# Weight conversions of a second MLP layer tied behind the last input copy, and the last output tile stored in halves on two queues

## Chip, cores and metric

One Trainium2 chip, one core of it. The metric is the device time of one execution in microseconds (us), of which the median of the runs is taken. The engines are TensorE (PE: matmuls; PEld: its weight loads), VectorE (DVE), ScalarE (ACT), GpSimd (POOL), and SyncE (SP), which issues the DMAs. The matrix of PE runs at one of two clock levels, and the profile shows the share that was granted.

## The reference

Attention over 4 batches, 12 heads, 448 positions and 64 channels, with RMS-normed queries and keys, is followed by two MLPs over the 1792 rows. The second MLP is where the change lies. Its weights are float64.

```python
def _moe_ref(x, w_in, w_out, s, b) -> np.ndarray:
    h = x @ w_in
    r = np.maximum(h, 0.0)
    g = s * (r * r) + b
    return (g @ w_out).astype(np.float32)

def _moe2_ref(x, w_in, w_out) -> np.ndarray:
    h = x @ w_in
    g = h * np.cos(h)
    return (g @ w_out).astype(np.float32)
```

Each x is 1792 x 768, each w_in 768 x 2048, each w_out 2048 x 768.

## The kernel before

Every fp32 operand of the MLPs is held as a high and a low part (`wh`, `wl` of a weight, `xh`, `xl` of an input, `gh`, `gl` of an activation), and each product is three matmuls (`products`). The weights come as 64-bit floats. `load_weight` (L435 on) loads each half of a weight, 128 x 384, as raw 64-bit words on SP's queue (L456, L458), takes the words apart with two ACT conversions, `c` (L468) and `t` (L469), joins them with three DVE passes (L472 to L474), casts the high part on ACT and subtracts on POOL (`halves`, L431 and L434). There are two raw buffers, two of `c`, three of `t`, and three of `wh` and of `wl`.

The second layer works in eight chunks of two tiles of the 2048 inner columns. For each tile and each of four batches there is an input unit (`unit_in`, L494 on): 18 matmuls into a PSUM buffer `ph`, of which there are three. ACT copies it out (`hs`, L523), and that frees the buffer; then ACT, DVE and POOL work out g = h cos(h) (`kk` L526 and L527, DVE L529 and L530, `gt` L531 and L532 on ACT and L533 on POOL, `gh` L534, `gl` L535). An output unit (`unit_out_2`, L574 on) is six matmuls of 128 rows by half of the 768 columns into a PSUM buffer `po`, of which there are three too. In the first chunk ACT copies `po` out (L590), in the others DVE adds it to the sum (L592). After the last chunk each of the 14 row tiles is stored (L600), in two pieces, since the rows of a tile lie in two places of the output.

`body` writes the program in the order of a list of units, with the weights `LOOK` = 8 units ahead (`ahead`). A scheduler that follows the dependencies then sets the order of each engine. `issue_after(later, earlier)` adds a dependency for the order alone: no semaphore is added. The first 16 weight halves are held behind certain exponentials of the attention in this way (`gate`); all later ones, those of the second layer among them, had no such tie.

Names in the rows of the order: `hs_2_1` is the copy of inner tile 2, batch 1; `c_4_1_0_1_0` is of segment 4 (the second layer), kind 1 (output weights; 0 is input weights), chunk or tile 0, column half 1, half 0.

Of the kernel before, what the change touches and what calls it, by code (L numbers as in the profile page):

```python
# [33 lines left out]
def body(ctx, tc, q, k, v, g_q, g_k, w1_in, w1_out, s_in, b_in, w2_in, w2_out, out):  # L34
    nc = tc.nc
    B, H, S, D = q.shape
    E = out.shape[1]
    F = w1_in.shape[1]
    P = 128
    NCH = 4  # L40
# [5 lines left out]
    NCK = NF // CF  # L46
    EH = E // 2
    CW = EH
    NT = 2 * S // P
# [35 lines left out]
    marks = {}  # L85
# [5 lines left out]
    def issue_after(later, earlier):  # L91
        info = mybir.DependencyInfo(mybir.DependencyClass.NoSync, mybir.DependencyReason.DATA)
        tc.add_manual_dep(later.ins, earlier.ins.name, info, reason="issue order")
# [342 lines left out]
    def load_weight(key):  # L436
        layer, seg, kind, a, e = key
        w = ((w1_in, w1_out), (w2_in, w2_out))[layer][kind]
        name = "_".join(map(str, key))
        wh = wp.tile([P, 2 * CW], F32R, tag="wh", name=f"wh_{name}", bufs=3)  # L440
        wl = wp.tile([P, 2 * CW], F32R, tag="wl", name=f"wl_{name}", bufs=3)
        weights[key] = wh, wl
        for o in range(2):
            kk = f"{name}_{o}"
            hi_part, lo_part = (z[:, o * CW:(o + 1) * CW] for z in (wh, wl))
            if (layer, kind, a, e, o) in plain:
                t = wp.tile([P, CW], F32, tag="t", name=f"t_{kk}", bufs=3)
                nc.sync.dma_start(t, plain[layer, kind, a, e, o])
                halves(t, hi_part, lo_part, nc.vector)
                continue  # L450
            own = "xb" in pools or count["raw"] % 3 < 2
            raw = (wp if own else pools["att"]).tile([P, CW], I64, tag="raw", name=f"raw_{kk}", bufs=2 if own else 1)
            count["raw"] += 1
            if kind == 0:
                src = w[o * CW:(o + 1) * CW, a * P:(a + 1) * P].rearrange("(c p) f -> p c f", p=P)
                dma = nc.sync.dma_start(raw.rearrange("p (c f) -> p c f", f=P), src)  # L456
            else:
                dma = nc.sync.dma_start(raw, w[(CF * a + o) * P:(CF * a + o + 1) * P, e * CW:(e + 1) * CW])  # L458
            if seg == 0 and kind == 0 and a == 0:
                follow(dma, marks["start"])  # L460
            ru = raw.bitcast(U32).rearrange("p (n two) -> p n two", two=2)
            lo, hi = ru[:, :, 0], ru[:, :, 1]
            c = wp.tile([P, CW], U32, tag="c", name=f"c_{kk}", bufs=2)
            cf = c.bitcast(F32)
            t = wp.tile([P, CW], U32, tag="t", name=f"t_{kk}", bufs=3)
            gate = GATE + 4 * min(count["raw"] - 1, 7) + 2 * max(count["raw"] - 8, 0)
            gate = min(gate, len(exps) - 1) if count["raw"] <= 16 else None
            for z in (nc.scalar.activation(cf, hi.bitcast(F32), AF.Copy, scale=2.0**-112),  # L468
                      nc.scalar.activation(t, lo, AF.Copy, scale=LSCALE, bias=-0.5)):  # L469
                if gate is not None:  # L470
                    issue_after(z, exps[gate])
            nc.vector.tensor_scalar(cf, cf, VMAX, -VMAX, ALU.min, ALU.max)  # L472
            nc.vector.scalar_tensor_tensor(t, c, 0x80000000, t, ALU.bitwise_and, ALU.bitwise_or)  # L473
            nc.vector.scalar_tensor_tensor(t, c, 3, t, ALU.logical_shift_left, ALU.bitwise_or)  # L474
            if layer == 0:
                d = dram.tile([P, CW], F32, tag=f"w_{kk}", name=f"wd_{kk}")
                nc.sync.dma_start(d, t.bitcast(F32))
                plain[layer, kind, a, e, o] = d
            halves(t.bitcast(F32), hi_part, lo_part, behind=exps[gate + 1] if count["raw"] <= 8 and gate + 1 < len(exps) else None)
# [3 lines left out]
    acc = {}  # L483
# [3 lines left out]
    def unit_in(layer, seg, ck, f, b):  # L487
        ft = ck * CF + f
        key = f"{layer}_{ft}_{b}"
        wh, wl = weights[layer, seg, 0, ft, 0]  # L490
        wh, wl = (z.rearrange("p (c f) -> p c f", f=P) for z in (wh, wl))
        pool, tag, bufs = (pools["psb"], "ph", 3) if "psb" in pools else (psm, "mo", 2)
        ph = pool.tile([P, 512], F32, tag=tag, name=f"ph_{key}", bufs=bufs)
        at = span(layer, seg, ck, b)  # L494
        size = at.stop - at.start
        h = ph[:, :size]

        def temp(pool, tag, name):
            return pool.tile([P, WIDE], F32, tag=tag, name=f"{name}_{key}")[:, :size]

        for c in range(NE):
            x = [z[:, at] for z in home(layer, b)[c]]
            for n, (a, m) in enumerate(products((wh[:, c, :], wl[:, c, :]), x)):
                nc.tensor.matmul(h, a, m, start=(c == 0 and n == 0), stop=(c == NE - 1 and n == 2))  # L504
            if c % 2 and c < NE - 1:
                yield 1.13
        if count["g"] % 2 == 0:
            n = count["g"] // 2
            gp, nb = (ma, 3) if "mb" not in pools or n % 5 < 3 else (pools["mb"], 2)
            pair[:] = [gp.tile([P, 2 * S], F32R, tag=f"g{z}", name=f"g{z}_{key}", bufs=nb) for z in "hl"]  # L510
        to = at if wide(layer, seg, ck) else slice(count["g"] % 2 * S, (count["g"] % 2 + 1) * S)
        gh, gl = (z[:, to] for z in pair)
        count["g"] += 1
        if layer == 0:
            r = temp(ma, "t0", "r")
            nc.scalar.activation(r, h, AF.Relu)  # L516
            r2 = temp(pools["mb"], "t1", "r2") if "mb" in pools else r
            nc.gpsimd.tensor_tensor(r2, r, r, ALU.mult)  # L518
            gt = temp(ma, "t2", "gt")
            nc.vector.tensor_scalar(gt, r2, sb[:, 0:1], sb[:, 1:2], ALU.mult, ALU.add)  # L520
        else:
            hs = temp(ma, "t0", "hs")
            nc.scalar.copy(hs, h)  # L523
            h = hs
            kk = temp(pools["mb"], "t1", "kk")
            nc.scalar.activation(kk, h, AF.Copy, scale=1.0 / (2 * math.pi), bias=MAGIC)  # L526
            nc.scalar.activation(kk, kk, AF.Copy, bias=-MAGIC)  # L527
            gt = temp(ma, "t2", "gt")
            nc.vector.scalar_tensor_tensor(gt, kk, -C1, h, ALU.mult, ALU.add)  # L529
            nc.vector.scalar_tensor_tensor(gt, kk, -C2, gt, ALU.mult, ALU.add)  # L530
            nc.scalar.activation(gt, gt, AF.Abs)  # L531
            nc.scalar.activation(gt, gt, AF.Sin, scale=-1.0, bias=halfpi)  # L532
            nc.gpsimd.tensor_tensor(gt, h, gt, ALU.mult)  # L533
        nc.scalar.copy(gh, gt)  # L534
        nc.gpsimd.tensor_tensor(gl, gt, gh.bitcast(F32), ALU.subtract)  # L535
        g[ft, b] = (gh, gl)
        if layer == 1 and b % 2:
            g[ft, "pair", b // 2] = list(pair)
        yield 1.13
# [36 lines left out]
    def unit_out_2(seg, ck, eh, t):  # L576
        key = f"1_{ck}_{eh}_{t}"
        w = [z.rearrange("p (f e) -> p f e", f=CF) for z in weights[1, seg, 1, ck, eh]]
        pr, j0 = t // NT, t % NT * P
        po = po_tile(key)[:, :EH]  # L580
        for f in range(CF):
            x = [z[:, j0:j0 + P] for z in g[ck * CF + f, "pair", pr]]
            for n, (a, m) in enumerate(products(x, [z[:, f, :] for z in w])):
                nc.tensor.matmul(po, a, m, start=(f == 0 and n == 0), stop=(f == CF - 1 and n == 2))  # L584
        if ck == 0 and eh == 0:
            pool, nb = (ma, NE) if t < NE else (pools["mb"], 2 * NT - NE)
            acc[t] = pool.tile([P, E], F32, tag="acc", name=f"acc_{key}", bufs=nb)
        at = acc[t][:, eh * EH:(eh + 1) * EH]
        if ck == 0:
            nc.scalar.copy(at, po)  # L590
        else:
            nc.vector.tensor_tensor(at, po, at, ALU.add)  # L592
        if ck < NCK - 1 or eh == 0:
            return
        j = j0
        while j < j0 + P:
            b, c, p = 2 * pr + j // S, j % S // CP, j % CP
            n = min(CP - p, j0 + P - j)
            rows = out[b * S:(b + 1) * S, :].rearrange("(p c) e -> c p e", c=NCH)[c, p:p + n, :]
            nc.sync.dma_start(rows, acc[t][j - j0:j - j0 + n, :])  # L600
            j += n

    pools["ps"] = att_scope.enter_context(tc.tile_pool(name="ps", bufs=2, space=PSUM))
# [87 lines left out]
    for n, u in enumerate(units):  # L691
# [24 lines left out]
        for cost in (unit_in if u[0] == "in" else unit_out)(*u[1:]):  # L716
            debt += cost * rates[min(seg, 1)]
            while debt > 0:
                c = next(steps, None)
# [34 lines left out]
```

## Time and profile before

| what | us |
|---|---|
| median of 3 runs | 1271.97 (1271.52 to 1272.73) |
| the profiled execution, own time | 1274.62 |
| its span, first to last instruction | 1272.7 |
| PE busy | 1239.8 (97%) |
| DVE, ACT, POOL busy | 854.2, 758.5, 624.7 |

The page of the profile gives the busy time and share of each engine, the chain that ended last and the costliest groups of instructions. Since PE is busy for nearly all of the span, the views to read are those that show where it waits and where its clock is lower. A group's idle time is that of its engine just before it, with what ended the wait.

### The profile page before, as it was taken

The page shows a single profiled execution, that of the slowest core. Times are in us where ns is not written, and L with a number is a line of the kernel's source. Part 1 is how long each engine was busy: PE and PEld are TensorE (multiplying, and loading weights), DVE is VectorE, ACT ScalarE, POOL GpSimd, SP SyncE. Part 2 cuts the span into 40 slices and gives each one's busy share as a digit, 9 for nine tenths or more (in the row PEclk, how much of TensorE's full clock was granted, in tenths as well). Part 3 has the DMA queues.
Part 4 walks back from the last instruction along what each step waited for, and adds up shares of the span by engine and source line. Part 5 has one row for each costly group of instructions (what it writes and reads, how often), then busy time and mean ns, then how long its engine had stood idle before and what let it go on. Part 6 is the DMA issues. An engine that isn't in the chain of part 4 may idle for free.

```text
span 1272.7 us, 19065 instructions
## 1 busy us (share of the span) xinstructions
PE 1239.8 (97%) x6788; PEld 1042.6 (82%) x6788; DVE 854.2 (67%) x1448; ACT 758.5 (60%) x1704; POOL 624.7 (49%) x681
## 2 busy tenths in 40 slices
PE   7999999999999999999999999899999999999998
PEld 5555676676877777889999999799899999999998
DVE  6888778878778674753454447754767766666755
ACT  5777887776667664435332226688656657566741
POOL 4566857575655526434332223555443545354531
PEclk9999999899999999999999999999999999999999
DMA  4323325434334343453222112211112111111105
GB/s 124 103 83 120 114 78 158 146 104 132 117 114 125 101 117 95 143 157 95 83 65 62 51 45 75 75 50 51 53 47 75 50 50 50 50 50 50 53 10 174
DMA packets 82222, 111.33 MB, mean 87 GB/s; under 512 B 8112, under 2 KB 72144, under 8 KB 82128
## 3 DMA queue, kind: packets, MB, share of 16 engines
q1 hardware_dynamic: 82128, 110.13, 28.6%
q8 instruction: 53, 0.87, 0.3%
q14 instruction: 41, 0.34, 0.1%
HBM read 86.51 MB, written 23.59 MB: 87 GB/s over the span
## 4 chain that ended last, share of the span: by engine, by line
PE 64%; DVE 7%; ACT 6%; DMA 2%; POOL 2%; issue 1%; DVEq 0%; ACTq 0%; POOLq 0%
PE ph L504 26%; PE po L558 15%; PE po L584 14%; PE tp L306 3%; PE av L329 3%; PE sc L265 3%; DVE gt L529 1%; DVE t L473 1%; DVE gt L530 1%; DVE t L474 1%; DVE c L472 1%; POOL wl L434 1%; DMA raw<-in_moe_w_out_dram 1%; DMA raw<-in_moe_w_in_dram 1%; DMA xr<-xd 1%
## 5 line engine op out<-in xcount | busy, mean ns | idle before, releaser
L535 POOL TENSOR_TENSOR gl<-gt,gh 128x448 fp32r<-128x448 f32 (+2 forms) x128 | 155.3, 1220 | 155.2 <-ACT gh L534 155.1
L504 PE MATMUL ph<-xha,wh 128*128 128x448 f32 (+2 forms) x576 | 212.3, 371 | 3.6 <-ACT hs L523 3.4
L504 PE MATMUL ph<-xha,wl 128*128 128x448 f32 (+2 forms) x576 | 211.1, 367 | 0.0
L504 PE MATMUL ph<-xla,wh 128*128 128x448 f32 (+2 forms) x576 | 210.7, 367 | 0.0
L434 POOL TENSOR_TENSOR wl<-t,wh 128x384 fp32r<-128x384 f32 x128 | 139.5, 1105 | 61.4 <-ACT wh L431 58.7
L431 ACT CAST wh<-t 128x384 fp32r<-128x384 f32 x200 | 95.6, 512 | 107.9 <-PE po L558 52.2
L566 DVE TENSOR_TENSOR acc<-po,acc 128x448 f32<-128x448 f32 x168 | 103.2, 618 | 83.8 <-PE po L558 83.8
L558 PE MATMUL po<-gh,wh 128*128 128x448 f32 x384 | 145.8, 382 | 8.5 <-DVE acc L566 6.4
L584 PE MATMUL po<-wh,gh 128*128 128x384 f32 x448 | 151.6, 339 | 1.7 <-DVE acc L592 1.5
L584 PE MATMUL po<-wl,gh 128*128 128x384 f32 x448 | 150.1, 335 | 0.4 <-POOL wl L434 0.4
L584 PE MATMUL po<-wh,gl 128*128 128x384 f32 x448 | 150.3, 335 | 0.0
L592 DVE TENSOR_TENSOR acc<-po,acc 128x384 f32<-128x384 f32 x196 | 105.3, 551 | 62.3 <-PE po L584 62.0
L558 PE MATMUL po<-gh,wl 128*128 128x448 f32 x384 | 141.1, 367 | 0.4 <-POOL wl L434 0.4
L287 ACT ACTIVATE pr<-sc,top 112x448 f32<-112x448 f32 x184 | 116.4, 640 | 41.3 <-DVE top L279 40.7
L558 PE MATMUL po<-gl,wh 128*128 128x448 f32 x384 | 140.8, 367 | 0.0
L533 POOL TENSOR_TENSOR gt<-hs,gt 128x512 f32<-128x512 f32 x64 | 76.0, 1194 | 123.8 <-ACT gt L532 115.4
L473 DVE SCALAR_TENSOR_TENSOR t<-c,t 128x384 uint32<-128x384 uint32 x128 | 99.8, 783 | 46.5 <-ACT t L469 43.6
L279 DVE TENSOR_REDUCE top<-sc 112x1 f32<-112x448 f32 x192 | 111.7, 615 | 18.0 <-PE sc L265 17.7
L504 PEld LDWEIGHTS ph<-xha,wh 128*128 128x128 f32 x576 | 108.7, 189 | 17.7 <-ACT hs L523 3.8
L518 POOL TENSOR_TENSOR r<-r 128x448 f32<-128x448 f32 x64 | 63.7, 996 | 120.3 <-ACT r L516 119.6
L534 ACT CAST gh<-gt 128x448 fp32r<-128x448 f32 (+2 forms) x128 | 71.4, 567 | 85.1 <-DVE gt L520 52.2
L504 PEld LDWEIGHTS ph<-xla,wh 128*128 128x128 f32 x576 | 108.6, 189 | 9.0 <-issue 0.6
(109 smaller groups left out, 2701.7 us busy)
## 6 DMA issues: line engine op xcount, KB each, us to landing
raw<-in_moe_w_in_dram SPq DMA_DIRECT2D x64, 384.0 KB, 3.4
raw<-in_moe_w_out_dram SPq DMA_DIRECT2D x64, 384.0 KB, 3.3
t<-wd SPq DMA_DIRECT2D x72, 192.0 KB, 2.4
wd<-t SPq DMA_DIRECT2D x64, 192.0 KB, 2.9
rawk<-in_k_dram SPq DMA_DIRECT2D x24, 224.0 KB, 3.7
rawv<-in_v_dram SPq DMA_DIRECT2D x24, 224.0 KB, 3.0
rawq<-in_q_dram SPq DMA_DIRECT2D x23, 224.0 KB, 3.5
xd<-xf SPq DMA_DIRECT2D x12, 224.0 KB, 3.0
```

The source lines that it names most:

```text
L279: line("DVE", nc.vector.tensor_reduce(tops[j], sc[j], axis=AX.X, op=ALU.max, negate=True))
L287: e = line("ACT", nc.scalar.activation(pr, sc[j], AF.Exp, bias=tops[j], scale=scale[j], accum_out=st[i]["sums"][:, c, j:j + 1]))
L431: z = nc.scalar.copy(wh, w)
L434: eng.tensor_tensor(wl, w, wh.bitcast(F32), ALU.subtract)
L473: nc.vector.scalar_tensor_tensor(t, c, 0x80000000, t, ALU.bitwise_and, ALU.bitwise_or)
L504: nc.tensor.matmul(h, a, m, start=(c == 0 and n == 0), stop=(c == NE - 1 and n == 2))
L533: nc.gpsimd.tensor_tensor(gt, h, gt, ALU.mult)
L535: nc.gpsimd.tensor_tensor(gl, gt, gh.bitcast(F32), ALU.subtract)
L558: marks["out"] = nc.tensor.matmul(po, a, m, start=(f == 0 and n == 0), stop=(f == CF - 1 and n == 2))
L566: nc.vector.tensor_tensor(at, po, at, ALU.add)
L584: nc.tensor.matmul(po, a, m, start=(f == 0 and n == 0), stop=(f == CF - 1 and n == 2))
L592: nc.vector.tensor_tensor(at, po, at, ALU.add)
```

## The change

Two things. First, each ACT conversion of a raw weight that has no other tie is now ordered behind the last `hs` copy that `body` had written until then. Second, the last row tile (t = 13) is stored in column halves: each half after its own last addition, and of its two pieces the first goes on SP's queue and the second on ACT's. Before, it was stored whole after both additions, both pieces on SP's queue.

```diff
@@ -469,6 +469,8 @@
                       nc.scalar.activation(t, lo, AF.Copy, scale=LSCALE, bias=-0.5)):
                 if gate is not None:
                     issue_after(z, exps[gate])
+                elif "hs" in marks:
+                    issue_after(z, marks["hs"])
@@ -520,7 +522,7 @@
             hs = temp(ma, "t0", "hs")
-            nc.scalar.copy(hs, h)
+            marks["hs"] = nc.scalar.copy(hs, h)
             h = hs
@@ -590,14 +592,17 @@
-        if ck < NCK - 1 or eh == 0:
+        closing = t == 2 * NT - 1
+        if ck < NCK - 1 or eh == 0 and not closing:
             return
+        cols = slice(eh * EH, (eh + 1) * EH) if closing else slice(0, E)
         j = j0
         while j < j0 + P:
             b, c, p = 2 * pr + j // S, j % S // CP, j % CP
             n = min(CP - p, j0 + P - j)
-            rows = out[b * S:(b + 1) * S, :].rearrange("(p c) e -> c p e", c=NCH)[c, p:p + n, :]
-            nc.sync.dma_start(rows, acc[t][j - j0:j - j0 + n, :])
+            rows = out[b * S:(b + 1) * S, :].rearrange("(p c) e -> c p e", c=NCH)[c, p:p + n, cols]
+            queue = nc.scalar if closing and j > j0 else nc.sync
+            queue.dma_start(rows, acc[t][j - j0:j - j0 + n, cols])
             j += n
```

The order of the four engines is as before up to the border of the two layers. Lines after L471 have moved by two, and those after L593 by up to five.

ACT at the border, before: the copy `hs_0_2` and what stands ahead of it.

```order
L534 CAST gh_1_0_9042<-gt_1_1_9135 128x384
L469 ACTIVATE t_4_1_0_0_1_9169<-raw_4_1_0_0_1_9166 128x384
L469 ACTIVATE t_4_1_0_1_0_9454<-raw_4_1_0_1_0_9451 128x384
L468 ACTIVATE c_4_1_0_1_1_9464<-raw_4_1_0_1_1_9462 128x384
L468 ACTIVATE c_4_0_3_0_0_9613<-raw_4_0_3_0_0_9611 128x384
L523 COPY hs_0_2_9218<-ph_0_2_9197 128x512
```

The same place now:

```order
L431 CAST wh_4_0_2_0_9087<-t_4_0_2_0_0_9092 128x384
L431 CAST wh_4_0_2_0_9087<-t_4_0_2_0_1_9103 128x384
L536 CAST gh_1_0_9042<-gt_1_0_9049 128x512
L109 CAST xha_96<-acc_0_5_2_7263 128x448
L533 ACTIVATE gt_1_1_9135<-gt_1_1_9135 128x384
L469 ACTIVATE t_4_1_0_0_1_9169<-raw_4_1_0_0_1_9166 128x384
L534 ACTIVATE gt_1_1_9135<-gt_1_1_9135,halfpi 128x384
L536 CAST gh_1_0_9042<-gt_1_1_9135 128x384
L525 COPY hs_0_2_9218<-ph_0_2_9197 128x512
```

Three conversions have left the place ahead of `hs_0_2`; one, `t_4_1_0_0_1`, stands two places further ahead, and the `wh` casts stand ahead of both `gh`.

POOL at the same place, now:

```order
L535 TENSOR_TENSOR gt_1_0_9049<-hs_1_0_9044,gt_1_0_9049 128x512
L434 TENSOR_TENSOR wl_4_0_2_0_9088<-t_4_0_2_0_0_9092,wh_4_0_2_0_9087 128x384
L434 TENSOR_TENSOR wl_4_0_2_0_9088<-t_4_0_2_0_1_9103,wh_4_0_2_0_9087 128x384
L537 TENSOR_TENSOR gl_1_0_9043<-gt_1_0_9049,gh_1_0_9042 128x512
L535 TENSOR_TENSOR gt_1_1_9135<-hs_1_1_9130,gt_1_1_9135 128x384
```

Before, `gl_1_0` and `gt_1_1` stood ahead of the two `wl`.

ACT behind the copy of unit (2, 1), now, where the conversions that were ahead of `hs_0_2` stand (`acc<-po` are the copies out of PSUM):

```order
L525 COPY hs_2_1_9382<-ph_2_1_9363 128x384
L468 ACTIVATE c_4_1_0_1_0_9453<-raw_4_1_0_1_0_9451 128x384
L469 ACTIVATE t_4_1_0_1_0_9454<-raw_4_1_0_1_0_9451 128x384
L468 ACTIVATE c_4_1_0_1_1_9464<-raw_4_1_0_1_1_9462 128x384
L469 ACTIVATE t_4_1_0_1_1_9465<-raw_4_1_0_1_1_9462 128x384
L528 ACTIVATE kk_2_0_9352<-hs_2_0_9350 128x512
L592 COPY acc_0_0_4_9438<-po_0_0_4_9431 128x384
L528 ACTIVATE kk_2_1_9384<-hs_2_1_9382 128x384
L529 ACTIVATE kk_2_0_9352<-kk_2_0_9352 128x512
L431 CAST wh_4_1_0_1_9449<-t_4_1_0_1_0_9454 128x384
L592 COPY acc_0_0_5_9447<-po_0_0_5_9440 128x384
```

Before, `hs_2_1` was followed by `kk_2_0`, the copy of `po_0_0_6` and the rest of `kk`, with no conversion among them.

## Rows read from the trace of the kernel before

**Rows 1.** The page, part 1: PE's busy time, share, instructions.

```profile
PE 1239.8 (97%) x6788; PEld 1042.6 (82%) x6788; DVE 854.2 (67%) x1448; ACT 758.5 (60%) x1704; POOL 624.7 (49%) x681
```

**Rows 2.** Table by stretch: length, busy time of engines, granted clock (PEclk), DMA.

```profile
800.00:820.00 20.00, 16.62 (x79) 14.24 (x78) 15.55 (x22) 12.45 (x26) 10.46 (x9) 0.97 0.15 41
820.00:840.00 20.00, 20.00 (x102) 18.82 (x101) 15.20 (x20) 17.23 (x38) 10.82 (x9) 0.94 0.27 79
840.00:860.00 20.00, 20.00 (x109) 19.05 (x109) 9.08 (x12) 17.85 (x41) 12.87 (x12) 1.00 0.15 41
```

**Rows 3.** Waits of PE from 800 us: total, times, longest.

```profile
PE ph L504 <- ACT hs L523: 3.4, 1, 3.4
PE po L584 <- DVE acc L592: 1.5, 3, 0.7
PE po L584 <- POOL wl L434: 0.4, 1, 0.4
```

**Rows 4.** Timeline of PE, the hole: start, us, what, idle before.

```profile
815.62 0.40 PE L504 MATMUL ph<-xla,wh 128*128 128x512 f32 x1
819.40 0.69 PE L504 MATMUL ph<-xha,wh 128*128 128x384 f32 x1 [3.38 <-ACT hs L523]
...
822.43 0.34 PE L504 MATMUL ph<-xha,wh 128*128 128x384 f32 x1
...
822.78 0.33 PE L504 MATMUL ph<-xla,wh 128*128 128x384 f32 x1
```

**Rows 5.** Timeline of ACT ahead of the late copy.

```profile
811.84 0.51 ACT L534 CAST gh<-gt 128x384 fp32r<-128x384 f32 x1
...
814.03 0.56 ACT L469 ACTIVATE t<-raw 128x384 uint32<-128x384 uint32 x1 [0.80 <-POOL wl L434]
816.48 0.55 ACT L468 ACTIVATE c<-raw 128x384 f32<-128x384 f32 x1 [1.89 <-DMA raw<-in_moe_w_out_dram]
818.33 0.54 ACT L468 ACTIVATE c<-raw 128x384 f32<-128x384 f32 x1 [1.30 <-DMA raw<-in_moe_w_in_dram]
818.78 0.57 ACT L523 COPY hs<-ph 128x512 f32<-128x512 f32 x1
```

**Rows 6.** Timeline of POOL at the same time.

```profile
810.26 1.02 POOL L533 TENSOR_TENSOR gt<-hs,gt 128x384 f32<-128x384 f32 x1 [2.70 <-ACT gt L532]
811.24 2.76 POOL L434 TENSOR_TENSOR wl<-t,wh 128x384 fp32r<-128x384 f32 x2
813.96 1.34 POOL L535 TENSOR_TENSOR gl<-gt,gh 128x384 fp32r<-128x384 f32 x1
```

**Rows 7.** Timeline of PE: one of the small waits.

```profile
969.40 0.45 PE L584 MATMUL po<-wh,gh 128*128 128x384 f32 x1 [0.68 <-DVE acc L592]
```

**Rows 8.** Table by stretch: the stretch with that wait.

```profile
950.00:1000.00 50.00, 49.32 (x264) 46.25 (x263) 35.01 (x64) 32.22 (x62) 22.41 (x20) 1.00 0.19 59
```

**Rows 9.** Groups from 816 to 1268 us: count, busy, mean ns, idle before, releasers.

```profile
L468 ACT ACTIVATE c<-raw 128x384 f32<-128x384 f32 x55 | 30.3, 551 | 31.5 <-DMA raw<-in_moe_w_out_dram 13.2 <-DMA raw<-in_moe_w_in_dram 7.3 <-DVE t L474 4.8
L473 DVE SCALAR_TENSOR_TENSOR t<-c,t 128x384 uint32<-128x384 uint32 x56 | 46.8, 836 | 30.5 <-ACT t L469 29.1
```

**Rows 10.** Timeline of ACT: a copy out of PSUM in the first chunk.

```profile
848.87 0.47 ACT L590 COPY acc<-po 128x384 f32<-128x384 f32 x1
```

**Rows 11.** Timeline of PE: the next use of that PSUM buffer.

```profile
851.05 0.33 PE L584 MATMUL po<-wh,gh 128*128 128x384 f32 x1
```

**Rows 12.** The page, part 6: loads of raw weights, KB, us to landing.

```profile
raw<-in_moe_w_in_dram SPq DMA_DIRECT2D x64, 384.0 KB, 3.4
```

**Rows 13.** Timeline of DVE: the last addition.

```profile
1268.00 0.56 DVE L592 TENSOR_TENSOR acc<-po,acc 128x384 f32<-128x384 f32 x1 [0.48 <-PE po L584]
```

**Rows 14.** Timeline of SP's queue: the first store after it.

```profile
1268.59 0.31 SPq L600 DMA_DIRECT2D out_dram<-acc  x1
```

**Rows 15.** DMA issues from 1266 us: count, KB, us to landing.

```profile
out_dram<-acc SPq DMA_DIRECT2D x1, 336.0 KB, 2.8
out_dram<-acc SPq DMA_DIRECT2D x1, 96.0 KB, 1.8
```

## The prediction

> **What bounds the kernel now.** I read the shares of the engines first. TensorE (PE) is busy for 1239.8 of the 1272.7 us [rows 1], so only what makes PE wait, or run slower, or what lies outside its work, can be won. Next I read the table by stretch across the border of the two layers. From 800 to 820 us PE is busy 16.62 of 20 us, and from 820 to 840 it is busy throughout, but at a granted clock of 0.94 and with 102 matmuls, where the next 20 us hold 109 [rows 2]. Then the list of who waited for whom, from 800 us on: one wait of 3.4 us for `hs` on ScalarE (ACT), three of 1.5 us together for VectorE (DVE), one of 0.4 us for GpSimd (POOL) [rows 3]. So the second layer has one large hole, and the timeline shows it: PE starts a matmul at 815.62 and the next at 819.40, with 3.38 us idle; nine starts later, at 822.43, full pace is back [rows 4].
>
> The hole has two prices. The wait itself is 3.38 us. After it the nine matmuls from 819.40 to 822.43 take 3.03 us, where two later starts from 822.43 to 822.78 are 0.175 us apart, so nine should take 1.58: 1.45 us more. Their pace is that of the lower of the two clock levels (1.2 against 2.4 GHz). Together **4.83 us**.
>
> Why `hs` is late stands on ACT's own timeline [rows 5]. The cast `gh` ends at 812.35. Then four conversions of weights stand ahead of `hs`: two wait for POOL (they start at 814.03 at the latest), two for a load of raw weights (1.89 and 1.30 us of idle time; they start at 816.48 and 818.33), and `hs` starts only at 818.78. ACT works in order, so a copy that frees a PSUM buffer for PE stands behind transfers that it does not need.
>
> **The change, part by part.**
>
> *The tie.* Every layer-two conversion now stands behind the last `hs` written ahead of it. By the order of instructions, one conversion is left between the `gh` work and the `hs` in question, and it waits for POOL's earlier casts alone; the two that waited for loads are gone from there. What is late next is POOL: its new order puts both `wl` and a `gl` ahead of the `gt` that the last `gh` ahead of `hs` needs. If the pair starts where it did, at 811.24, then 2.76 (pair) + 1.34 (`gl`) + 1.02 (`gt`) [rows 6] end at 816.4; `gh` and `hs` add 0.51 and 0.57 [rows 5], so `hs` ends at 817.4. PE is free at about 816.0. That leaves 1.4 us of the wait. The `wh` casts that release the pair stand two places earlier on ACT now, worth 2 × 0.5, so 0.4 is left; at best it is nothing. I take 0.7, between 0.4 and 1.4 and nearer to the lower, and assume that the clock holds: the wait of 0.68 us at 969.40 lies in a stretch with a granted clock of 1.00 [rows 7, 8]. Won: 4.83 − 0.7 = **4.1 us**; ends 4.83 (no wait) and 3.38 − 1.4 = 2.0 (the clock falls all the same).
>
> *What is now behind the tie.* Of the conversions that were done before the hole, four now come after `hs` of unit (2, 1), in the stretch in which ACT also empties the output units' PSUM buffers (28 copies by the code, first chunk only). Each is 0.55 us [rows 9]: 2.2 us more work for ACT. ACT comes to the first `hs` about 2.7 us sooner (3.38 − 0.7), so it is 0.5 us ahead of the old program, while PE is 4.1 us ahead: PE comes 3.6 us closer to ACT. The cover is the time from a copy's end to the next use of its buffer, three output units on: at the tightest from 849.34 to 851.05, 1.7 us [rows 10, 11]. So 1.9 us would be missing, if ACT had no gaps; it has, 2.8 and 2.15 us in the two stretches of 20 us [rows 2]. Ends 0 and 1.9. I take **0.7 us lost**, nearer to the end with gaps, as a gap that waits for a load stays a gap.
>
> *Loads.* The raw tile has two buffers, so a load on SP's queue starts when the conversions two halves earlier are done. The same loads stand in the same order; they start later, and take 3.4 us [rows 12]. The tightest weight is that for input tile 3: from the matmul that ends unit (2, 1) to its first use PE has 79 matmuls of 384 columns (0.175 us each) and 18 of 512 (by columns 0.233), 18.0 us. The chain: two conversions free the buffer (1.1), load (3.4), four conversions (2.2), three DVE passes (0.84 each at the mean of the slowest kind [rows 9], 2.5), `wh` about 0.5, `wl` pair 2.76: 12.5 us. It is hidden; cost nothing, with 5.5 us to spare.
>
> *The last tile.* Before, DVE's last addition ends at 1268.56, the 48 KB store is issued at 1268.59 for 0.31 us, and the 336 KB one behind it, landing 2.8 us later [rows 13, 14]. Now half of both has left one unit earlier, and the last large store is 168 KB and issued on ACT's queue at once. The place in the queue gives 0.31 us. Landing lies between 1.8 us (96 KB) and 2.8 us (336 KB) [rows 15]; I take 2.2, by size nearer to 96 KB, and so 0.6. Sum **0.9 us**; ends 1.3 (landing as for 96 KB) and −0.3 (all lands as late as before, and a queue unused until then costs one more issue of 0.31). Two more stores are issued beside other work.
>
> The Trainium skill, "DMA: Bandwidth & Descriptors", section "Rules for kernel authors", speaks against this: stores from several engines share the same 16 DMA engines, so a second queue saves issue time alone. By it the tail would give 0.31 us and the sum below would be 3.7; the halving by time, one unit earlier, is a thing it does not speak of.
>
> *The small waits* of 1.5 and 0.4 us [rows 3] depend on DVE's and POOL's order, which moves everywhere in layer two. They may go or come again elsewhere: 0, ends +1.9 and −1.9.
>
> **Sum:** 4.1 − 0.7 + 0.9 = 4.3 us. The profiled execution's own time is 1274.62 (1272.7 of span and 1.9 around it), so it would be 1270.3; that execution is 2.65 us above the median of the runs, and against the median of 1271.97 the forecast is **1267.7 us**.
>
> **Rivals.**
> 1. *ACT becomes the bound in the first chunk.* The copies out of PSUM come late by the whole 3.6 us, because each gap waits for a load as before. For it: ACT is busy 17.23 and 17.85 of 20 us there, without the additions [rows 2]. Against it: PE is busy throughout in both stretches, so there is cover. Time: 4.1 − 3.6 + 0.9 = 1.4 us won, 1270.6.
> 2. *Slower: a weight comes late in every chunk.* In all seven chunks two weights now begin behind the second input copy. For it: the conversions already idle 20.5 us for loads [rows 9], and their cover falls to 18 us. Against it: a chain of 12.5 us. It decides once queueing behind other work on ACT and DVE adds over 5.5 us; at 1.5 us late seven times it costs 10.5 us: 1278.2.
> 3. *The last store lands no sooner after its issue.* The two halves are in flight on the same DMA engines within about one output unit, and the last 168 KB land 2.8 us after their issue, as 336 KB did [rows 15]. For it: size alone does not set the time, since 3.5 times the bytes of the 96 KB store took only 1.0 us more. Against it: the smaller store was the faster all the same. The tail gives the place in the queue, 0.31 us: 3.7 us won, 1268.3. The Trainium skill's rule named above comes to the same.
> 4. *Everything goes:* no wait is left at the hole (4.83), nothing is lost on ACT, tail 0.9, small waits gone (1.9): 7.6 us won, 1264.4.
>
> That the change does nothing is no rival: the order of instructions shows the conversions moved.
>
> **Numbers.** Chances: forecast 0.39, rival 1 0.23, rival 2 0.07, rival 3 0.15, rival 4 0.16. A measurement here tells 0.2% from no change, 2.5 us. Forecast, 3 and 4 lie below 1269.4: faster 0.70. Rival 1 lies within: same 0.23. Slower 0.07. The range leaves out rival 2 and the far side of rival 4, some 0.15, and takes in the bounds of the evacuation, the wait and the tail: 1264.6 to 1270.9.
>
> **What would show it.** Right: no wait for `hs` of over 1 us near 816 us, no stretch at 0.94, `hs` directly behind `gh` on ACT, and less than the 4.1 us (1272.7 − 1268.56) from DVE's last addition to the end. Rival 1 would show as PE waiting for the copies of the first chunk between 830 and 850 us; rival 2 as PE waiting for `wh` or `wl` once in every chunk. The prediction is wrong if the hole keeps over 2 us, or if waits of more than 2 us appear where none are now.

## The result and the profile after

| kernel | median, us | runs | ratio to before, 95% interval |
|---|---|---|---|
| before, beside the changed kernel | 1271.52 | 7 (1270.54 to 1278.24) | |
| changed | 1280.03 | 7 (1278.78 to 1285.55) | 1.0064 (1.0042 to 1.0087) |

The change makes the kernel slower by some 8 us. The forecast was 1267.7 us, its range 1264.6 to 1270.9, so the time lies outside and on the other side.

The profiled execution of the changed kernel has an own time of 1278.78 us, the fastest of its runs; that of before, 1274.62, is 3 us above its median. At the border, up to which the order is the same, the changed execution is already 2.9 us ahead: the first matmul whose place differs starts at 776.86 us in place of 779.76. So the two spans, 1277.0 and 1272.7, understate the loss, and the traces are compared by stretch.

**The hole is gone, as forecast.** First the same table by stretch as before [rows 2], of the changed kernel, from 800 to 860 us:

```profile
800.00:820.00 20.00, 19.82 (x97) 17.37 (x96) 13.60 (x20) 14.84 (x32) 12.23 (x10) 1.00 0.15 41
820.00:840.00 20.00, 20.00 (x110) 19.11 (x109) 11.62 (x20) 19.17 (x43) 10.01 (x10) 1.00 0.26 79
840.00:860.00 20.00, 20.00 (x108) 18.78 (x107) 12.98 (x17) 17.02 (x39) 11.43 (x10) 1.00 0.28 80
```

PE is busy for 19.82 us in place of 16.62, and the granted clock is 1.00 in all three rows. ACT's timeline at that place:

```profile
807.20 0.55 ACT L469 ACTIVATE t<-raw 128x384 uint32<-128x384 uint32 x1
810.63 0.51 ACT L536 CAST gh<-gt 128x384 fp32r<-128x384 f32 x1 [2.38 <-POOL gt L535]
811.05 0.58 ACT L525 COPY hs<-ph 128x512 f32<-128x512 f32 x1
```

`hs` starts directly behind `gh`, which waits for POOL's `gt` alone. Before, `hs` started at 818.78 [rows 5].

**New waits stand in the later chunks.** Whom PE waits for, from 790 us on (total, times, longest); before it was [rows 3]:

```profile
PE po L586 <- DVE acc L594: 7.5, 11, 2.5
PE po L586 <- POOL wl L434: 0.9, 1, 0.9
PE ph L506 <- DVE xla L110: 0.2, 1, 0.2
```

The waits for VectorE's additions have grown from 1.5 us in three to 7.5 us in eleven. The longest, on PE's timeline:

```profile
1142.33 0.34 PE L506 MATMUL ph<-xla,wh 128*128 128x384 f32 x1
1145.16 0.44 PE L586 MATMUL po<-wh,gh 128*128 128x384 f32 x1 [2.50 <-DVE acc L594]
...
1146.66 0.52 PE L586 MATMUL po<-wl,gh 128*128 128x384 f32 x1
...
1149.56 0.52 PE L586 MATMUL po<-wl,gh 128*128 128x384 f32 x1
```

and the table by stretch of what follows:

```profile
1146.00:1150.00 4.00, 4.00 (x16) 3.84 (x15) 3.88 (x6) 1.37 (x5) 2.13 (x2) 0.58 0.00 0
```

PE waits 2.50 us; 1.5 us after it has started again the clock falls, and ten matmuls from 1146.66 on take 0.32 us each in place of 0.174, 1.5 us more. VectorE's timeline tells why the addition was late:

```profile
1139.36 0.54 DVE L594 TENSOR_TENSOR acc<-po,acc 128x384 f32<-128x384 f32 x1
1139.83 0.90 DVE L475 SCALAR_TENSOR_TENSOR t<-c,t 128x384 uint32<-128x384 uint32 x1
1140.76 1.53 DVE L476 SCALAR_TENSOR_TENSOR t<-c,t 128x384 uint32<-128x384 uint32 x1
1142.22 1.16 DVE L474 TENSOR_SCALAR c<-c 128x384 f32<-128x384 f32 x1
1143.49 0.56 DVE L475 SCALAR_TENSOR_TENSOR t<-c,t 128x384 uint32<-128x384 uint32 x1
1144.08 0.56 DVE L476 SCALAR_TENSOR_TENSOR t<-c,t 128x384 uint32<-128x384 uint32 x1
1144.56 0.55 DVE L594 TENSOR_TENSOR acc<-po,acc 128x384 f32<-128x384 f32 x1
```

Five passes of weight conversions stand between two additions, and VectorE has hardly any idle time there (0.2 us). So here no weight is late: the engine that makes the weights is busy with them when it should empty a `po` buffer.

**How much, and where.** I summed over PE's matmuls the time from one start to the next less the matmul's own pace at full clock (0.1735 us for 384 columns, 0.2295 for 512, 0.206 for the few of 448): the lateness, which holds waits, slow clock and slow starts alike.

| stretch, us | 796–880 | 880–940 | 940–1000 | 1000–1060 | 1060–1120 | 1120–1180 | 1180–end | 880–end |
|---|---|---|---|---|---|---|---|---|
| before | 5.4 | 2.8 | 1.5 | 0.3 | 0.3 | 1.3 | 1.2 | 7.3 |
| changed | 0.9 | 2.9 | 4.1 | 1.6 | 2.2 | 4.7 | 4.3 | 19.7 |

The hole gives back 4.5 us, the later chunks lose 12.4. Of the 12.4, listed waits are 6.4 (2.0 to 8.4); each wait also slows the two starts beside it by some 0.27 us together, 2.2 us more for eight more waits; the fall of the clock is 1.5. Of the remaining 2.3, 0.8 are idle times under 0.15 us, thirteen in place of two, which the list of waits leaves out; the rest are slower starts that the profile gives no reason for.

**The tail** is shorter. VectorE's last addition, the last two stores and the landing of the stores (count, KB, median us):

```profile
1273.03 0.56 DVE L594 TENSOR_TENSOR acc<-po,acc 128x384 f32<-128x384 f32 x1 [0.49 <-PE po L586]
1273.61 0.31 SPq L605 DMA_DIRECT2D out_dram<-acc  x1
1273.62 0.38 ACTq L605 DMA_DIRECT2D out_dram<-acc  x1
```

```profile
out_dram<-acc ACTq DMA_DIRECT2D x2, 168.0 KB, 2.4
out_dram<-acc SPq DMA_DIRECT2D x2, 24.0 KB, 2.0
```

From the end of the last addition (1273.58) to the end of the span (1276.99) it is 3.41 us, before 4.19 (1268.56 to 1272.75): 0.78 won. In all, −4.5 + 12.4 − 0.8 = 7.1 us, beside 8.5 by the medians, whose interval is 5.3 to 11.1.

### The profile page after: what moved, and what is told of

Read it like the earlier page. It is cut to its first block, busy times and chain, and to the rows that moved or that the text cites. A ratio compares the mean times of both kernels' runs of the same rounds, so it can differ in the third digit from the quotient of the medians.

```text
span 1277.0 us, 19073 instructions
## 1 busy us (share of the span) xinstructions
PE 1242.4 (97%) x6788; PEld 1041.7 (82%) x6788; DVE 859.4 (67%) x1448; ACT 757.7 (59%) x1704; POOL 627.5 (49%) x681
## 4 chain that ended last, share of the span: by engine, by line
PE 61%; DVE 12%; ACT 6%; issue 2%; POOL 1%; DMA 1%; DVEq 0%; POOLq 0%; ACTq 0%
PE ph L506 24%; PE po L560 16%; PE po L586 12%; PE av L329 3%; PE tp L306 3%; PE sc L265 3%; DVE t L475 2%; DVE t L476 2%; DVE gt L531 2%; DVE c L474 2%; DVE gt L532 1%; DVE acc L594 1%; DMA xr<-xd 1%; ACT gh L536 1%; ACT kk L529 1%
## 5 line engine op out<-in xcount | busy, mean ns | idle before, releaser
L535 POOL TENSOR_TENSOR gt<-hs,gt 128x512 f32<-128x512 f32 x64 | 80.7, 1266 | 124.2 <-ACT gt L534 124.0
L506 PEld LDWEIGHTS ph<-xha,wl 128*128 128x128 f32 x576 | 108.2, 188 | 9.0 <-issue 0.3
```

## Experiments

The theory after the result: the ties push a chunk's conversions together behind an input copy; VectorE gets their passes in one burst, its additions come late, and with three `po` buffers PE waits. Rivals: the stores on the second queue; a loss set off at the border; weights that come late; the number of VectorE's passes. Ratios are to the kernel before, run beside each group. Where nothing else is said, an edit is shown against the changed kernel, cut down to the lines that matter.

**1. Which half of the change.** `e_tail` leaves out the tie; `e_tie` has the old store.

```diff
-                elif "hs" in marks:                                    # e_tail
-                    issue_after(z, marks["hs"])
...
-        if ck < NCK - 1 or eh == 0 and not closing:                    # e_tie
+        if ck < NCK - 1 or eh == 0:
...
-            queue = nc.scalar if closing and j > j0 else nc.sync
-            queue.dma_start(rows, acc[t][j - j0:j - j0 + n, cols])
+            nc.sync.dma_start(rows, acc[t][j - j0:j - j0 + n, :])
```

> The stored halves alone, without the tie. If the tie is the cause of the loss (theory), this kernel keeps the hole near 816 us and gains only what the trace of the changed kernel shows at its end: 4.14 us from the last addition to the end become 3.41, so 0.7 us less than before, about 1270.8, and no waits of PE for DVE's additions beyond the three of 1.5 us that were there. If the stores on ACT's queue were to blame, it is slower than before by over 2 us.

> The tie alone, with the last tile stored as before. Theory: the tie is the whole loss, so about 8.5 + 0.7 = 9 us slower than before, 1280.7, with waits of PE for DVE's additions in the later chunks of 7 us and more and no wait for the input copy near 816 us. Rival (the store is to blame): no slower than before, as the hole of 4.8 us is gone.

Measured: `e_tail` 1273.63, ratio 0.9995 (0.9974 to 1.0015): 0.7 us is below what this can tell, and a loss of over 2 us from the stores lies outside the interval. `e_tie` 1282.01, 1.0073 (1.0054 to 1.0092). The waits of `e_tail` from 796 us on:

```profile
PE ph L504 <- ACT hs L523: 3.3, 2, 3.0
PE po L584 <- DVE acc L592: 2.0, 4, 0.7
```

`e_tie` has the changed kernel's three lines of waits to the digit. On PE, VectorE, ACT and POOL the trace of `e_tail` has the order of the kernel before, that of `e_tie` the order of the changed kernel. The tie is the loss.

**2. Which weights.**

```diff
-                elif "hs" in marks:
+                elif "hs" in marks and (a // CF if kind == 0 else a) < 1 + (kind == 0):      # e_first
+                elif "hs" in marks and not ((a // CF if kind == 0 else a) < 1 + (kind == 0)):  # e_later
```

> The change with the tie kept only for the weights that are needed around the hole: output weights of chunk 0 and input tiles 0 to 3; later weights are free as before. Theory (the loss comes from the weights of the later chunks, whose VectorE passes are bunched behind the input copy): the hole stays closed (-4.8), the tail gains 0.7, and the later chunks wait as before, so about 5 us faster than before, 1266.5. Rival (the tie at the hole itself sets off the delays of all later chunks, for instance because POOL and DVE never catch up): within 2.5 us of the changed kernel, about 1279.

> The change with the tie only for the later weights (input tiles from 4 on, output chunks from 1 on). Theory: the hole of 4.8 us is back and the later chunks wait as in the changed kernel, so about 1280 + 4.8 = 1285, at least 1282. Rival (the loss is set off at the hole): the hole is back and nothing else, about 1271.

Measured: `e_first` 1265.91, 0.9946 (0.9928 to 0.9964); `e_later` 1285.13, 1.0100 (1.0079 to 1.0120). Both as the theory has them. Waits of `e_later`, from 796 us on:

```profile
PE po L586 <- DVE acc L594: 8.0, 14, 2.4
PE ph L506 <- ACT hs L525: 3.1, 1, 3.1
PE po L586 <- POOL wl L434: 0.9, 1, 0.9
```

and of `e_first`:

```profile
PE po L586 <- DVE acc L594: 1.0, 2, 0.9
PE po L586 <- POOL wl L434: 0.4, 1, 0.4
```

The hole and the loss are two places of one edit. The tie on the input weights of chunks 0 and 1 and the output weights of chunk 0 closes the hole; the tie on the others makes the waits, whether the hole is there or not. VectorE's and POOL's load in the same stretch shows the burst, of the changed kernel and then of `e_first` (columns as in [rows 2]; `e_first` is some 4 us ahead by then):

```profile
1000.00:1010.00 10.00, 10.00 (x54) 9.30 (x54) 6.34 (x13) 8.24 (x18) 3.97 (x5) 1.00 0.17 49
1010.00:1020.00 10.00, 10.00 (x55) 9.50 (x54) 9.89 (x14) 7.15 (x15) 9.18 (x6) 1.00 0.48 149
```

```profile
1000.00:1010.00 10.00, 10.00 (x55) 9.36 (x54) 9.31 (x18) 7.22 (x16) 3.83 (x3) 1.00 0.41 121
1010.00:1020.00 10.00, 10.00 (x58) 9.86 (x57) 5.60 (x12) 6.88 (x12) 5.11 (x5) 1.00 0.00 0
```

In the changed kernel VectorE is full (9.89 of 10) in the same 10 us in which POOL is (9.18), and the passes are then few and long: 14 instructions, where `e_first` does 18 in less time ten us sooner.

**3. Which of the later weights.**

```diff
-                elif "hs" in marks:
+                elif "hs" in marks and (kind == 0 or a < 1):          # e_in: input weights
+                elif "hs" in marks and (kind == 1 or a // CF < 2):    # e_out: output weights
```

> The changed kernel, with the output weights of chunks 1 to 7 left free; the input weights stay tied. By the order of instructions the second output weight of a chunk is then converted before the input copy, and 12 conversions in place of 16 stand behind it in a row. Theory (16 conversions in one burst fill VectorE for over 10 us while POOL is busy too, and the additions come late): a burst a quarter smaller leaves less than half of the 12 us that the changed kernel loses behind 880 us against the kernel before: at most 1274, and more likely 1268 to 1272. Rival (any conversion tied behind an input copy delays the weights, whichever): within 3 us of 1280.

> The opposite: input tiles from 4 on left free, the output weights tied. By the order of instructions the burst is the same as in the changed kernel, since the loads of the input weights stand behind the tied output weight in the two raw buffers. Theory: as slow as the changed kernel, 1278 to 1283, with the same waits for VectorE's additions, 7 to 8 us. Rival (the ties count by their number, half of them gone): about 1273.

Measured: `e_in` 1267.28, 0.9956 (0.9936 to 0.9976); `e_out` 1281.20, 1.0065 (1.0041 to 1.0090). Waits for VectorE's additions from 880 us on, of `e_in` and then of `e_out`:

```profile
PE po L586 <- DVE acc L594: 2.0, 3, 1.3
```

```profile
PE po L586 <- DVE acc L594: 7.6, 12, 2.5
```

`e_out` has in fact the changed kernel's order on every engine, row by row. So its run is a second measurement of the same program, and what it shows beyond that is in the order: beside those of the output weights, the ties of the later input weights bind nothing more. ACT's order in both, the copy of inner tile 8, batch 1, and what follows:

```
L525 COPY hs_8_1_11148<-ph_8_1_11129 128x384
L468 ACTIVATE c_4_1_3_1_0_11213<-raw_4_1_3_1_0_11211 128x384
L469 ACTIVATE t_4_1_3_1_0_11214<-raw_4_1_3_1_0_11211 128x384
L468 ACTIVATE c_4_1_3_1_1_11224<-raw_4_1_3_1_1_11222 128x384
L469 ACTIVATE t_4_1_3_1_1_11225<-raw_4_1_3_1_1_11222 128x384
```

The four conversions of a chunk's second output weight wait for this copy; the loads of the next three weights wait for their two raw buffers, and so all 16 conversions of a chunk stand between `hs_8_1` and `hs_9_0`, and none from there to `hs_10_1`. In `e_in` that weight is converted earlier, from just ahead of `hs_9_0` to just behind `hs_9_3` for the next chunk. By the order, then, it is the tie on these four conversions per chunk that sets off the loss. A kernel with that tie alone, in every chunk, was not run.

**4. Start or size.** `e_prev` ties the later weights behind the copy before the last:

```diff
-                    issue_after(z, marks["hs"])
+                    issue_after(z, marks["hs" if (a // CF if kind == 0 else a) < 1 + (kind == 0) else "hs0"])
...
-            marks["hs"] = nc.scalar.copy(hs, h)
+            marks["hs0"], marks["hs"] = marks.get("hs"), nc.scalar.copy(hs, h)
```

> The changed kernel, with the later weights tied behind the input copy before the last one, some 3.3 us of PE's time sooner. The burst is the same 16 conversions. Theory (the burst is the cause, not its exact start): still slow, 1276 to 1281. Rival (the conversions are just a few us too late for the weights): most of the loss is gone, 1272 or less.

Measured: 1274.43, 1.0011 (0.9996 to 1.0025); waits from 880 us on:

```profile
PE po L586 <- DVE acc L594: 6.7, 11, 1.5
PE po L586 <- POOL wl L434: 0.6, 1, 0.6
```

Between the two expectations, so neither is right by itself. The 16 conversions, one unit sooner, have nearly the same sum of waits, but none over 1.5 us, and lateness from 880 us on is 12.9 in place of 19.7. But the burst is not the same: between the input copies from the second of a chunk on, the changed kernel has 10, 2 and 4 conversions, `e_prev` from the first on 4, 7, 1 and 4. So it starts sooner and is also less dense, and this run does not separate the two.

**5. In its own chunk, or building up.** `e_one` adds one weight to `e_first` (shown against `e_first`):

```diff
-                elif "hs" in marks and (a // CF if kind == 0 else a) < 1 + (kind == 0):
+                elif "hs" in marks and ((a // CF if kind == 0 else a) < 1 + (kind == 0) or (kind, a, e) == (1, 4, 1)):
```

> The kernel with the tie on the first weights alone (1265.9), with the tie added for the second output weight of one later chunk, number 4: four conversions. Theory (each chunk's burst makes its own waits): between 1070 and 1095 us, behind the copy that they are tied to, waits for VectorE's additions appear that the kernel without this tie hasn't got there, and before that its times and waits are the same; cost about a sixth of the 12 us, 1 to 3 us, so 1267 to 1269. Rival (the delay builds up over chunks): no waits there, within 0.5 us of 1265.9.

Measured: 1271.92, 0.9981 (0.9967 to 0.9995); by the ratios 4.4 us slower than `e_first`, more than the 1 to 3 expected. Lateness of the two, by the stretches of the first table:

| stretch, us | 880–940 | 940–1000 | 1000–1060 | 1060–1120 | 1120–1180 | 1180–end | 880–end |
|---|---|---|---|---|---|---|---|
| `e_first` | 0.7 | 0.3 | 0.3 | 0.4 | 1.6 | 1.1 | 4.4 |
| `e_one` | 1.4 | 0.2 | 0.3 | 2.0 | 2.9 | 2.1 | 9.0 |

The jump of 1.6 us stands in the chunk of the tie, with this wait on PE's timeline:

```profile
1080.11 0.45 PE L586 MATMUL po<-wh,gh 128*128 128x384 f32 x1 [0.47 <-DVE acc L594]
```

So the burst acts where it is, as expected. But another 2.3 us come later. There the orders differ too: from 1027 us to the end the scheduler has remade the order of the engines, so this isn't shown to be a delay that builds up. That part stays open. (The 0.7 us ahead of 940 stand where both programs have the same order: that much two executions differ.)

**6. What makes the additions late.** `e_noclamp` leaves out, for the tied weights, the pass of L474 (the limit to the largest fp32 value). `e_wlv` moves the subtraction for `wl` from POOL to VectorE.

```diff
-            nc.vector.tensor_scalar(cf, cf, VMAX, -VMAX, ALU.min, ALU.max)                           # e_noclamp
+            if layer == 0 or "hs" not in marks:
+                nc.vector.tensor_scalar(cf, cf, VMAX, -VMAX, ALU.min, ALU.max)
...
-            halves(t.bitcast(F32), hi_part, lo_part, behind=...)
+            halves(t.bitcast(F32), hi_part, lo_part, nc.vector if "hs" in marks else nc.gpsimd, behind=...)  # e_wlv
```

> The changed kernel without the clamp, the first of the three VectorE passes over each weight half, for the weights of the second layer that are tied (the computation leaves out the limit to the largest fp32 value). Theory (a burst of VectorE passes stands ahead of the additions): a burst a third shorter leaves less than half of the 7.5 us of waits, since a wait is only what exceeds the slack of three buffers, and the time falls by 5 us or more, to 1275 or below. Rival (the conversions are late through the tie and their loads): the passes are not what is waited for, and the time stays within 3 us of 1280.

> The changed kernel with the subtraction for the low part of a layer-two weight on VectorE in place of POOL, so that POOL has 1.38 us less work for each half and VectorE one pass more. If the burst hurts because VectorE's passes stretch from 0.55 to 1.2 to 1.6 us while POOL works (theory, its second part), the passes of the burst run nearer to 0.55 us, and the waits for the additions fall in spite of the added pass: under 4 us, time 1274 or less. If it is VectorE's number of passes alone that counts, a pass more per half (a quarter more) makes it worse: over 1282.

Measured: `e_noclamp` 1272.63, 0.9998 (0.9982 to 1.0014), with 8.1 us of waits in nine. The time fell as expected, the waits did not, so a third fewer passes did not lower them. Its VectorE, ahead of a wait of 1.59 us:

```profile
1009.46 0.55 DVE L595 TENSOR_TENSOR acc<-po,acc 128x384 f32<-128x384 f32 x1
1009.93 1.34 DVE L477 SCALAR_TENSOR_TENSOR t<-c,t 128x384 uint32<-128x384 uint32 x1
1011.20 1.37 DVE L532 SCALAR_TENSOR_TENSOR gt<-kk,hs 128x384 f32<-128x384 f32 x1
1012.60 1.25 DVE L533 SCALAR_TENSOR_TENSOR gt<-kk,gt 128x384 f32<-128x384 f32 x1
1013.78 1.65 DVE L476 SCALAR_TENSOR_TENSOR t<-c,t 128x384 uint32<-128x384 uint32 x1
1015.46 1.38 DVE L477 SCALAR_TENSOR_TENSOR t<-c,t 128x384 uint32<-128x384 uint32 x1
1016.76 0.55 DVE L595 TENSOR_TENSOR acc<-po,acc 128x384 f32<-128x384 f32 x1
```

Five operations that take 0.55 us each elsewhere take 1.25 to 1.65 here, 6.8 us from the first start to the next addition. `e_wlv`: 1272.08, 1.0000 (0.9985 to 1.0015), waits of 4.2 us in six (under 4 were expected). VectorE has a pass more per weight half (four in place of three) and the time still fell by 8 us against the changed kernel. The groups of the two remaining t passes from 880 to 1260 us, of the changed kernel and then of `e_wlv`:

```profile
L475 DVE SCALAR_TENSOR_TENSOR t<-c,t 128x384 uint32<-128x384 uint32 x48 | 36.1, 752 | 6.6 <-ACT t L469 5.5
L476 DVE SCALAR_TENSOR_TENSOR t<-c,t 128x384 uint32<-128x384 uint32 x48 | 35.5, 742 | 0.4
```

```profile
L476 DVE SCALAR_TENSOR_TENSOR t<-c,t 128x384 uint32<-128x384 uint32 x48 | 31.6, 661 | 0.3
L475 DVE SCALAR_TENSOR_TENSOR t<-c,t 128x384 uint32<-128x384 uint32 x48 | 28.3, 589 | 0.0
```

The passes became shorter, 752 to 589 ns and 742 to 661, as POOL had less to do. So VectorE's count of passes alone does not set the waits, and the stretch beside POOL's work has a part in them: the five passes from 1139.83 us on, ahead of the longest wait of the changed kernel, take 4.7 us, and at 0.55 each (0.35 for the limit) would take 2.6. Of the 7.5 us of waits in the changed kernel, 5.7 are six waits with 0.8 us or more of such stretch between the awaited addition and the one before it. But the tie did not bring the stretch as such: in the kernel before, the same two passes take 849 and 754 ns on the mean of the same 380 us, no less than in the changed kernel, beside 1.9 us of waits; only the limit is longer now, 608 ns in place of 410. What differs ahead of these waits is that the stretched passes stand together. The order moved too in both kernels, so neither fall of 8 us can be put down to its edit alone, and the shares of stretch and place are not separated.

**7. More `po` buffers.** Three kernels rotate over five buffers, two of them idle before: the changed kernel, `e_first` and the kernel before.

```diff
-        pool, tag, bufs = (pools["psb"], "po", 3) if "psb" in pools else (psm, "mo", 2)
+        count["po"] = count.get("po", 0) + 1
+        pool, tag, bufs = (psm, "mo", 2) if "psb" not in pools or count["po"] % 5 > 2 else (pools["psb"], "po", 3)
```

> The changed kernel with five PSUM buffers for the output units in place of three (the two more stand idle in the second layer). Theory (VectorE's additions come late in bursts, and PE waits because all three buffers are still full): the burst is ridden out, the waits for the additions fall from 7.5 us to under 2, the clock stays at its upper level after 880 us, and the time falls by 8 us or more, to 1272 or below, near the 1266 of the kernel with the tie on the first weights alone. Rival (a weight that is late, or VectorE short of time on the average): PE then waits for the weight, or for the additions all the same, and the time stays within 3 us of 1280.

> The tie on the first weights alone, with five PSUM buffers for the output units. Theory: what is left there to win are the 1.0 us of waits for VectorE's additions, so 0.5 to 1.5 us less than 1265.9, hardly to be told from it. If it is slower, the order that the scheduler makes with more buffers has a price of its own.

> The control: the kernel before with five PSUM buffers for the output units. It has 1.5 us of waits for VectorE's additions, so by the theory it gains 1 to 3 us (about 1271 beside 1273), far less than the changed kernel gains from the same edit. If it gains as much as the changed kernel, the buffers are a gain of their own and say nothing of the tie.

Measured: changed 1267.29, 0.9960 (0.9944 to 0.9976); `e_first` 1273.78, 1.0005 (0.9989 to 1.0022); before 1265.12, 0.9938 (0.9923 to 0.9952). The changed kernel gains 13 us, but its waits are 4.7 us, not under 2; the control gains 8 in place of 1 to 3; and `e_first` loses nearly 8. The control has no listed wait of PE left from 880 us on. With more buffers the scheduler makes another order, from 579 us on (in the first layer already), and each of the three got its own. As a test of the buffers it is inconclusive.

**8. The fastest.** The kernel before with five buffers, as in 7, and the split store; no tie (shown against the changed kernel):

```diff
-                elif "hs" in marks:
-                    issue_after(z, marks["hs"])
...
-        pool, tag, bufs = (pools["psb"], "po", 3) if "psb" in pools else (psm, "mo", 2)
+        count["po"] = count.get("po", 0) + 1
+        pool, tag, bufs = (psm, "mo", 2) if "psb" not in pools or count["po"] % 5 > 2 else (pools["psb"], "po", 3)
```

> The kernel before with five PSUM buffers for the output units and with the last tile stored in halves over two queues: no tie at all. The order of the engines is that of the kernel with five buffers up to the last unit, so it should be that kernel's time (1265.1) less the 0.7 us that the tail gave in the changed kernel: 1264.4, and 3.4 us from the last addition to the end. If the split store has a price of its own, it is slower than 1265.1.

Measured: 1263.84, 0.9925 (0.9903 to 0.9947), the fastest of all, but not to be told from the same kernel without the split store. The order of the engines is that of the control in 7. From the last addition to the end it is 4.31 us, not 3.4, beside 4.65 without the split: a gain of 0.3. The other twelve traces with the split store have 3.39 to 3.55 us there, and the other two without it 4.19, so this tail is an exception that stays open.

## Why the prediction was wrong

- **The hole: right.** Forecast 4.1 us won; the lateness from 796 to 880 us went from 5.4 to 0.9, 4.5 us. The rest of 0.7 us that I left there did not appear: POOL's `wl` pair came at 804.94, not 811.24, and `hs` ended at 811.6 in place of 817.4; 2.9 us of both is the lead that this execution had at the border, the rest is sooner than forecast. The price of 4.83 us holds for the profiled execution of before: in `e_tail`, which has the same order, the hole's wait of 3.00 us was followed by no low clock, so the 1.45 us for the clock are not lost every time.
- **Copies out of PSUM in the first chunk: 0.7 us lost, measured none.** PE is busy throughout from 820 to 860 us, so rival 1 did not come about either.
- **Loads and weights: hidden, right.** No wait for a weight but the one for `wl`, 0.9 us, that was 0.4 before. Rival 2's price of 10.5 us is near the loss, but its mechanism is not what happened: no weight was waited for once in every chunk. It also counted two weights per chunk behind the second input copy; the order has all four, 16 conversions.
- **The tail: right.** 0.9 us forecast, 0.78 in this pair of profiles: the last store is issued 0.35 us sooner behind the last addition, the place in the queue, and lands 2.28 us after its issue in place of 2.78; from its landing to the end it is 0.08 more. The Trainium skill, "DMA: Bandwidth & Descriptors", section "Rules for kernel authors", gives issue time alone: here that accounts for under half, and the greater part goes with the last store being half as large (168 in place of 336 KB). In the pair of experiment 8 only 0.3 remained.
- **The step that failed** is that of the small waits: "They may go or come again elsewhere: 0, ends +1.9 and −1.9." Its lower end stopped at the waits that were there to lose; the term is −12.4 us. I followed the tied conversions on ACT and their loads, in the first chunk only, where ACT empties `po`. In the other seven it is VectorE that empties it, and the releaser in [rows 3] is its addition; each tied weight half brings it three passes, the slowest kind 0.84 us [rows 9]. That group also said why there had been room: VectorE stood idle for 30.5 us ahead of that pass, nearly all of it waiting for ACT; from 880 to 1260 us it was 20.9:

```profile
L473 DVE SCALAR_TENSOR_TENSOR t<-c,t 128x384 uint32<-128x384 uint32 x47 | 39.9, 849 | 20.9 <-ACT t L469 19.7
```

In the changed kernel it is 6.6 there (the group L475 above): the slack that kept passes and additions apart is gone. VectorE's load is nearly the same in that stretch, 257.4 us busy before and 261.5 now; the tie moved its idle time, it did not fill it.
- The order of the engines, from which the forecast was made at the border, showed the 16 conversions between the second and the fifth input copy of every later chunk. I didn't price it.

## What to carry to other kernels

A tie for the order alone works on every later instance of the code it stands in, and on every load queued behind it: price the steady state, not only the place that is to be mended, and tie no more than that place needs (here 1265.9 in place of 1280.0). Before work is moved together, look on every engine downstream for what else it does in that time, above all for what frees a buffer. When a scheduler makes the order, a small edit can remake all of it: the one edit of experiment 7 moved three kernels by −13, +8 and −8 us. So a control with the same edit on the kernel before is needed.

## What was not expected of the hardware

VectorE's additions, which read one operand from PSUM, hold 550 ns in every kernel; passes of the same 384 columns with both operands in SBUF run from 0.55 to 1.65 us, the long ones beside POOL's work. In the changed kernel from 880 to 1260 us, the 25 of the 48 passes of L475 that POOL overlaps for under 5% of their time take 0.54 to 0.56 us each; the 16 that POOL overlaps for over half of their time take 1.09 on the mean, up to 1.65. The 53 additions that POOL overlaps in this way take 550 ns like the rest. The group of the additions in the changed kernel from 880 to 1260 us:

```profile
L594 DVE TENSOR_TENSOR acc<-po,acc 128x384 f32<-128x384 f32 x183 | 98.4, 550 | 63.1 <-PE po L586 63.1
```

The Trainium skill, "SBUF — State Buffer", section "Who interferes with whom", has this rule: an instruction of VectorE with two inputs in SBUF contends with one of GpSimd that reads SBUF, one with at most one input there, outside the two-port modes, does not. The traces agree for the additions and these passes (550 ns beside means of 742 to 849). The limit of L474 has a single input in SBUF and is not spared: 0.35 us without POOL, 1.04 on the mean of the 18 that POOL overlaps for over half of their time. Whether it runs in a two-port mode no run here shows.

What a wait costs beyond itself isn't fixed by its length. The wait of 2.4 to 2.5 us near 1145 us was followed by a low clock in each of four executions (changed, `e_tie`, `e_out`, `e_later`): ten or eleven matmuls, 1.5 us, from 0.4 to 1.5 us after PE had started again. A wait of 1.59 us near 958 us in `e_tie` had the same sequel, as this row of the table by stretch shows (granted clock 0.79; eleven matmuls, 1.7 us), and so had the same wait in `e_out`:

```profile
958.00:966.00 8.00, 6.36 (x26) 5.72 (x26) 7.93 (x13) 4.79 (x11) 4.42 (x4) 0.79 0.47 142
```

The profile of the changed kernel has that wait too, 1.60 us from the same place, and its clock stayed at 1.00 from 950 to 1000 us; so did the clock of `e_noclamp` behind its three waits of 1.59 and 1.60, and that of `e_tail` behind the 3.00 us at the hole. That the clock did not fall there may be part of why the profiled execution of the changed kernel is its fastest; it isn't shown. What decides between the two I can't tell from these runs.
